# Each store as two transfers of 64 rows: a grouped 1x1 convolution on Trainium2

## The chip, the cores and the metric

The kernel runs on one core of a Trainium2 chip. The metric is the device time of one execution in microseconds (us). Before the change it is 492.37 us (median of 2 runs, 492.31 and 492.43).

## The reference, cut to what matters

The input is an image of 512 x 512 pixels with 192 bf16 channels. The kernel size is 1, so each of four groups of 48 channels is multiplied by its own 48 x 48 matrix (shortened, with k = 1 filled in):

```python
H = W = 512; G = 4; Cg = 48; C = 192; k = 1
xg = xp.reshape(B, H, W, G, Cg)
out = out + jnp.einsum('bhwgc,gcd->bhwgd', xg, w[0, 0])     # once, as k = 1
```

That is 100.7 MB in and 100.7 MB out with little arithmetic.

## The kernel before

Pixels are laid out so that each of the 128 partitions holds a contiguous run of pixels. The 2048 pixel columns per partition are moved in pieces. Most have 64 columns, which is 3 MB: 128 rows of 24,576 bytes. At both ends there are five smaller pieces. SP (SyncE) issues the loads, ACT (ScalarE) the stores. TensorE (PE) transposes pixels, multiplies them by the weights, and writes to PSUM; DVE (VectorE) copies the transposed data, and ACT and DVE evict the results, that is, copy them from PSUM to SBUF. Input and output each have a ring of 256 columns, four pieces. A piece of the output ring may be overwritten only when its store has landed, that is, when its semaphore has reached the count that the code waits for, 16 for each store (the trace has 16 landings for each).

```python
def rows_view(ap, p):
    return ap[128 * p.col:128 * (p.col + p.size), :].rearrange("(p i) c -> p (i c)", p=128)
...
for p in stores:
    seen[p.key] = seen.get(p.key, 0) + 16
    st_val[p] = seen[p.key]
...
def wait_out_free(wq, g):                      # ACT and DVE, before an eviction
    if g >= body:                              # body: 64 groups, the whole ring
        p = store_at[g - body]
        wq.wait(st_sem[p.key], st_val[p])
...
# SP
for p in loads:
    wq.wait(t_done, p.g1 - body)
    sp.dma_start(ring_view(x_sb, p), rows_view(xf, p)).then_inc(ld_sem[p.key], 16)
...
# ACT
def store(p):
    act.dma_start(rows_view(of, p), ring_view(o_sb, p)).then_inc(st_sem[p.key], 16)

for g in range(NG):
    wait_out_free(wq, g)
    wq.wait(mm_done, g + 1)
    while pending and pending[0][1] <= g:
        store(pending.pop(0)[0])
    ...                                        # evict group g
    if g in store_end:
        pending.append((store_end[g], g + ST_DELAY))
```

Of the kernel before, what the change touches and what calls it, by code (L numbers as in the profile page):

```python
# [67 lines left out]
def bass_standalone__grouped__vision_kernel(nc, x, w, out):  # L68
# [14 lines left out]
    of = out.rearrange("b h w c -> (b h w) c")  # L83
# [9 lines left out]
    def shared(g):  # L93
        return g % 4 == 1 and g < NG - 3
# [9 lines left out]
    def rows_view(ap, p):  # L104
        return ap[128 * p.col:128 * (p.col + p.size), :].rearrange("(p i) c -> p (i c)", p=128)

    def ring_view(t, p):
        at = p.col % RCOLS
        assert at + p.size <= RCOLS
        return t[:, at * C:(at + p.size) * C]  # L110

    with ExitStack() as es:
        block = es.enter_context(nc.Block())
        x_sb = es.enter_context(nc.sbuf_tensor("x_sb", [128, RCOLS * C], BF16))
        o_sb = es.enter_context(nc.sbuf_tensor("o_sb", [128, RCOLS * C], BF16))
# [8 lines left out]
        def sem(name):  # L124
            return es.enter_context(nc.semaphore(name))

        ld_sem = {k: sem(f"ld_{k[0]}{k[1]}") for k in dict.fromkeys(p.key for p in loads)}
        st_sem = {k: sem(f"st_{k[0]}{k[1]}") for k in dict.fromkeys(p.key for p in stores)}
        st_val, seen = {}, {}
        for p in stores:  # L130
            seen[p.key] = seen.get(p.key, 0) + 16
            st_val[p] = seen[p.key]
        w_sem, id_sem, e_sem, wb_sem, wc_sem = (sem(s) for s in ("w_sem", "id_sem", "e_sem", "wb_sem", "wc_sem"))
        p0_sem, p1_sem = sem("p0_sem"), sem("p1_sem")
# [5 lines left out]
        def wait_out_free(wq, g):  # L140
            if g >= body:
                p = store_at[g - body]
                wq.wait(st_sem[p.key], st_val[p])

        @block.gpsimd
        def _(gp):
            gp.memset(esel[:], 1.0).then_inc(p0_sem, 1)  # L147
            gp.memset(ident[:], 1.0).then_inc(p1_sem, 1)  # L148
            gp.wait_ge(p0_sem, 1)
            gp.affine_select(out=esel[:], in_=esel[:], pattern=[[-1, ECOLS]],  # L150
                             compare_op=AluOpType.is_equal, fill=0.0, base=ESHIFT,
                             channel_multiplier=1).then_inc(e_sem, 1)
            gp.wait_ge(p1_sem, 1)
            gp.affine_select(out=ident[:], in_=ident[:], pattern=[[-1, 128]],  # L154
                             compare_op=AluOpType.is_equal, fill=0.0, base=0,
                             channel_multiplier=1).then_inc(id_sem, 1)
# [101 lines left out]
        @block.scalar  # L258
        def _(act):
            wq = Waiter(act)  # L260
            pending = []

            def store(p):
                act.dma_start(rows_view(of, p), ring_view(o_sb, p)).then_inc(st_sem[p.key], 16)  # L264

            for g in range(NG):
                wait_out_free(wq, g)
# [3 lines that stand above are left out]
                v = 2 * g  # L271
                u = g % body * 2
                if shared(g):
                    ins = act.copy(o_sb[:, u * UC:(u + 1) * UC], o_ps[:, v % NOB, 0:UC])  # L274
                else:
                    dst = o_sb[:, u * UC:(u + 2) * UC].rearrange("p (u c) -> p u c", u=2)
                    ins = act.copy(dst, o_ps[:, v % NOB:v % NOB + 2, 0:UC])  # L277
                ins.then_inc(fa_sem[g % RING], 1)
                if g in store_end:
                    pending.append((store_end[g], g + ST_DELAY))  # L280
            for (p, _) in pending:
                act.wait_ge(fa_sem[(p.g1 - 1) % RING], 1)
                store(p)
            for p in stores:
                if st_val[p] == seen[p.key]:
                    wq.wait(st_sem[p.key], st_val[p])
# [28 lines left out]
```

## Time and profile before

| | before |
|---|---|
| time, span of the profiled run | 492.37 us, 489.8 us |
| bytes moved | 201.6 MB |
| middle of the run (106 to 425 us) | DMA share 1.00, 431 GB/s |
| a row of 24,576 bytes | one packet, 912 ns (median), so 26.9 GB/s in each of 16 engines |
| store issues on ACT | 40 of 338 ns, 13.7 us in total |

The packet durations are from the trace's records of single packets, which the views below only sum up. From the page of the kernel before: the DMA share and rate in 40 slices of the span, the two queues (packets, MB, share of 16 engines' time; q1 has the loads, q10 the stores), the chain that ended last by engine and by line, and the large issues (count, KB, us to landing).

```profile
span 489.8 us, 14171 instructions
...
DMA  8999999999999999999999999999999999998593
GB/s 297 430 425 423 428 430 433 427 435 425 436 425 432 433 431 433 429 432 431 425 433 430 429 435 429 434 429 433 429 429 426 438 421 434 421 424 351 238 385 149
...
q1 hardware_dynamic: 5968, 100.68, 48.3%
q10 hardware_dynamic: 5760, 100.67, 48.2%
...
DMA 77%; PE 18%; ACT 1%; another core or an unknown queue 1%; issue 1%; SPq 1%; ACTq 0%
DMA out_dram<-o_sb 73%; PE o_ps L215 10%; PE xT_ps L192 8%; DMA x_sb<-in_x_dram 4%; ACT o_sb L277 1%; SPq L164 0%; ACTq L264 0%; SPq L161 0%; ACTq L46 0%
...
out_dram<-o_sb ACTq DMA_DIRECT2D x30, 3072.0 KB, 45.4
```

The DMA slices stay at 9 of 10 nearly to the end, at about 430 GB/s, with loads and stores half each. The chain is 73% stores. A store takes 45.4 us to land, though 3 MB alone would take 7.3 us at 431 GB/s: it stands in a queue behind earlier stores (in the middle they land 15.2 us apart, three in its 45.4), and shares the engines with loads (48.3% and 48.2% of their time).

The stretches view gives, for stretches of the span, the busy time of each engine, then the granted PE clock, the DMA share and the rate:

```profile
106.00:425.00 319.00, 277.20 (x4032) 268.47 (x4032) 221.08 (x421) 233.49 (x337) 0.00 (x0) 0.95 1.00 431
...
460.00:490.00 30.00, 16.80 (x227) 15.53 (x226) 10.99 (x21) 15.07 (x21) 0.00 (x0) 0.84 0.54 224
```

PE is busy for 277 of 319 us there and ACT for 233, so both have slack. DMA has none. Waits by engine (total us, times, longest) show what the queue does to the others:

```profile
ACT o_sb L277 <- DMA out_dram<-o_sb: 46.9, 23, 2.8
PE o_ps L215 <- ACT o_sb L277: 44.8, 25, 2.7
```

Last, ACT's timeline at one store (start, us; ACTq is its issue):

```profile
348.72 0.80 ACT L277 CAST o_sb<-o_ps 128x768 bf16<-128x768 f32 x1 [2.75 <-DMA out_dram<-o_sb]
348.73 0.34 ACTq L264 DMA_DIRECT2D out_dram<-o_sb  x1
```

ACT waited 2.75 us for a store to land. The issue of the next store took 0.34 us and ran under an eviction.

### The profile page before, as it was taken

What the parts mean: (1) busy time and instruction counts of PE and PEld (TensorE: products, weight loads), DVE (VectorE), ACT (ScalarE), POOL (GpSimd) and SP (SyncE); (2) the same over time, 40 slices, a digit from 0 to 9 for tenths busy, and PEclk for the clock granted to TensorE, in tenths of its full rate; (3) what the DMA queues carried; (4) which work ended last, traced back from release to release, by engine and by line L of the source; (5) the groups of instructions that cost most, each with busy time, mean ns of one, the idle gap of its engine ahead of it and who ended that gap; (6) DMA issues with size and microseconds to landing.
All of it is one profiled execution on the core that took longest, in us unless ns stands there. A gap on an engine that the chain in (4) does not pass through costs nothing.

```text
span 489.8 us, 14171 instructions
## 1 busy us (share of the span) xinstructions
PE 423.4 (86%) x6154; PEld 407.9 (83%) x6154; DVE 336.1 (69%) x640; ACT 357.2 (73%) x513; POOL 1.3 (0%) x8
## 2 busy tenths in 40 slices
PE   5999989977997979979798979899798979799962
PEld 5899989977987879878788878898787978799862
DVE  3688878867675767757676757767577757588750
ACT  2788878866785767767677757678586868688862
POOL 1000000000000000000000000000000000000000
PEclk9999999999898998989998989989899989899996
DMA  8999999999999999999999999999999999998593
GB/s 297 430 425 423 428 430 433 427 435 425 436 425 432 433 431 433 429 432 431 425 433 430 429 435 429 434 429 433 429 429 426 438 421 434 421 424 351 238 385 149
DMA packets 11750, 201.63 MB, mean 412 GB/s; under 512 B 1488, under 2 KB 2512, under 8 KB 3536
## 3 DMA queue, kind: packets, MB, share of 16 engines
q1 hardware_dynamic: 5968, 100.68, 48.3%
q10 hardware_dynamic: 5760, 100.67, 48.2%
q8 instruction: 12, 0.20, 0.1%
q14 instruction: 10, 0.08, 0.0%
HBM read 100.68 MB, written 100.66 MB: 411 GB/s over the span
## 4 chain that ended last, share of the span: by engine, by line
DMA 77%; PE 18%; ACT 1%; another core or an unknown queue 1%; issue 1%; SPq 1%; ACTq 0%
DMA out_dram<-o_sb 73%; PE o_ps L215 10%; PE xT_ps L192 8%; DMA x_sb<-in_x_dram 4%; ACT o_sb L277 1%; SPq L164 0%; ACTq L264 0%; SPq L161 0%; ACTq L46 0%
## 5 line engine op out<-in xcount | busy, mean ns | idle before, releaser
L277 ACT CAST o_sb<-o_ps 128x768 bf16<-128x768 f32 x385 | 301.7, 799 | 116.8 <-PE o_ps L215 68.4
L249 DVE COPY xT_sb<-xT_ps 128x768 bf16<-128x768 bf16 x512 | 284.0, 555 | 111.4 <-PE xT_ps L192 104.4
L215 PE MATMUL o_ps<-wt,xT_sb 128*128 128x144 bf16 (+1 forms) x3072 | 308.2, 238 | 47.9 <-ACT o_sb L277 44.8
L192 PE MATMUL xT_ps<-ident,x_sb 128*128 128x128 bf16 x3072 | 265.7, 225 | 7.8 <-DMA x_sb<-in_x_dram 7.3
L215 PEld LDWEIGHTS o_ps<-wt,xT_sb 128*128 128x128 bf16 x3072 | 217.8, 100 | 61.4 <-issue 52.5
L192 PEld LDWEIGHTS xT_ps<-ident,x_sb 128*128 128x128 bf16 x3072 | 205.6, 101 | 9.5 <-DMA x_sb<-in_x_dram 7.6
L255 DVE CAST o_sb<-o_ps 128x384 bf16<-128x384 f32 x127 | 69.8, 550 | 28.0 <-DMA out_dram<-o_sb 26.7
L274 ACT CAST o_sb<-o_ps 128x384 bf16<-128x384 f32 x127 | 61.0, 480 | 8.0 <-PE o_ps L215 5.1
L245 DVE CAST wt<-o_ps 128x480 bf16<-128x480 f32 x1 | 0.7, 658 | 3.2 <-PE o_ps L176 3.2
L176 PE MATMUL o_ps<-w_sb,esel 48*128 48x48 bf16 x10 | 0.6, 210 | 2.6 <-DMA w_sb<-in_w_dram 2.6
L176 PEld LDWEIGHTS o_ps<-w_sb,esel 48*128 48x128 bf16 x10 | 0.5, 112 | 2.5 <-POOL esel L150 2.5
L277 ACT ACT_TABLE_LOAD x1 | 1.3, 1283 | 0.8 <-PEq L300 0.8
L150 POOL TENSOR_SCALAR_AFFINE_SELECT esel<-esel 48x272 bf16<-48x272 bf16 x1 | 0.4, 406 | 0.0
L147 POOL MEMSET esel<- 48x272 bf16 x1 | 0.3, 318 | 0.3 <-POOLq L300 0.3
L154 POOL TENSOR_SCALAR_AFFINE_SELECT ident<-ident 128x128 bf16<-128x128 bf16 x1 | 0.3, 285 | 0.0
L148 POOL MEMSET ident<- 128x128 bf16 x1 | 0.2, 198 | 0.0
L300 POOL MEMSET const-bfloat16-1.0<- 128x1 bf16 x1 | 0.1, 102 | 0.0
L300 POOL MEMSET const-uint8-127<- 128x1 uint8 x1 | 0.1, 102 | 0.0
L300 POOL MEMSET const-float32-0.0<- 128x1 f32 x1 | 0.1, 98 | 0.3 <-issue 0.3
L300 POOL MEMSET const-float32-1.0<- 128x1 f32 x1 | 0.1, 98 | 0.0
## 6 DMA issues: line engine op xcount, KB each, us to landing
x_sb<-in_x_dram SPq DMA_DIRECT2D x30, 3072.0 KB, 25.7
out_dram<-o_sb ACTq DMA_DIRECT2D x30, 3072.0 KB, 45.4
x_sb<-in_x_dram SPq DMA_DIRECT2D x2, 1536.0 KB, 19.7
out_dram<-o_sb ACTq DMA_DIRECT2D x2, 1536.0 KB, 24.9
x_sb<-in_x_dram SPq DMA_DIRECT2D x2, 768.0 KB, 21.5
out_dram<-o_sb ACTq DMA_DIRECT2D x2, 768.0 KB, 20.0
x_sb<-in_x_dram SPq DMA_DIRECT2D x4, 192.0 KB, 27.2
x_sb<-in_x_dram SPq DMA_DIRECT2D x2, 384.0 KB, 24.4
```

Source lines behind the costliest of these rows:

```text
L147: gp.memset(esel[:], 1.0).then_inc(p0_sem, 1)
L150: gp.affine_select(out=esel[:], in_=esel[:], pattern=[[-1, ECOLS]], compare_op=AluOpType.is_equal, fill=0.0, base=ESHIFT, channel_multipli ...
L154: gp.affine_select(out=ident[:], in_=ident[:], pattern=[[-1, 128]], compare_op=AluOpType.is_equal, fill=0.0, base=0, channel_multiplier=1) ...
L176: last = pe.matmul(o_ps[:, NOB - 1, col:col + CG], lhsT=esel[:, s0:s0 + 128], rhs=w_sb[:, g, :], start=True, stop=True, skip_group_check=True)
L192: ins.append(pe.transpose(xT_ps[:, g % NXP, j * 128:(j + 1) * 128], x_sb[:, col:col + 128], ident[:]))
L215: ins.append(pe.matmul(o_ps[:, v % NOB, c0_:c1_], lhsT=xs[:, j * 128:(j + 1) * 128], rhs=wt[:, WOFF[tc]:WOFF[tc] + (c1_ - c0_)], start=(tc ...
L245: dve.tensor_copy(wt[:], o_ps[:, NOB - 1, 0:WCOLS]).then_inc(wc_sem, 1)
L249: dve.tensor_copy(xT_sb[g % NXP][:], xT_ps[:, g % NXP, 0:2 * UC]).then_inc(e1_sem[g % RING], 1)
L255: dve.tensor_copy(o_sb[:, u * UC:(u + 1) * UC], o_ps[:, v % NOB, 0:UC]).then_inc(d2_sem[g // 4 % 2], 1)
L274: ins = act.copy(o_sb[:, u * UC:(u + 1) * UC], o_ps[:, v % NOB, 0:UC])
L277: ins = act.copy(dst, o_ps[:, v % NOB:v % NOB + 2, 0:UC])
L300: nc = _bacc.Bacc("TRN2", target_bir_lowering=False, num_devices=1)
```

## The change

Each store is issued as two transfers, rows 0 to 63 and rows 64 to 127, on the same queue. The intent of such a split is usually smaller units that start and finish separately. Here the wait still needs both.

```diff
         for p in stores:
-            seen[p.key] = seen.get(p.key, 0) + 16
+            seen[p.key] = seen.get(p.key, 0) + 32
             st_val[p] = seen[p.key]
...
             def store(p):
-                act.dma_start(rows_view(of, p), ring_view(o_sb, p)).then_inc(st_sem[p.key], 16)
+                for r in (0, 64):
+                    act.dma_start(rows_view(of, p)[r:r + 64, :], ring_view(o_sb, p)[r:r + 64, :]).then_inc(st_sem[p.key], 16)
```

## The prediction

> **What bounds the kernel now.** The 16 DMA engines. The page's slices show DMA at 0.9 or more from slice 2 to 37 and about 430 GB/s; the stretches view gives DMA share 1.00 and 431 GB/s from 106 to 425 us. The queue table splits it evenly: loads 48.3%, stores 48.2% of 16 engines. The chain of waits is 73% store transfers, in links of 45.5 us: a store is about three pieces deep in its queue, and its landing frees the output ring for ACT (46.9 us of waits) and DVE (26.7 us). A 24,576-byte row is one packet of 912 ns in the trace's DMA records: 26.9 GB/s per engine, 16 of them 431. PE (86%) and ACT (73%) have slack.
>
> **What the change does directly.** Bytes and row length stay the same, so data packets stay the same. Each store gets a second set of 16 completion packets: 640 more at 9 ns over 16 engines is 0.4 us. ACT issues 40 more transfers at 338 ns (13.5 us in total), where it idles 27%; I put 0 to 3 us of it on the chain. Completion is not earlier, since the wait needs both halves. There is nothing to gain.
>
> **What it does indirectly, the main term.** A 128-row store reads all of SBUF; a 64-row one reads half. [...] The trace before has no large 64-row transfer, so no run shows it yet. [...]
>
> Stores are half the traffic (215 GB/s)[...]. But an engine alternates load and store packets[...]. Let T be 0.91 us. A load and store pair takes 2T now; [...] engines that lag by over half a store (4 packet pairs, 7.3 us) read different halves. One engine already lands up to 20 us behind, the rest within 2 to 5 us. So I expect 1.15 to 1.4 times over the roughly 390 us in which both queues run, and some 5 to 15 us at the end, where only stores run.
>
> Estimate: 492 + 0.25 × 390 + 10 = 600 us. Range 494 to 710; the top is 1.5 times throughout. Faster 1%, within 2% 26%, slower 73%.
>
> **What would show it.** Right: store packets' mean well over 918 ns, towards 1.2 to 1.8 us, with load packets near 915; DMA share still near 1.0 in the middle but GB/s down to 290 to 380; PE and ACT idle more, waiting on stores; the store links of the chain longer than 45.5 us; the same number of data packets and 6,400 packets on the store queue. If the store packets stay at 912 ns, [...] the time should be within 1% of before.
>
> **What would make it wrong.** [...] the engines settling into opposite phases by themselves, load on one and store on the other.

The sum came to 600 us: 492 as measured, 0.25 × 390 = 98 for the middle, and 10 for the end. Terms are cut from the text, with the cuts marked: why a 64-row store should be slower, and the model that led to 1.15 to 1.4 times, to 1.5 times at the top and to the 5 to 15 us at the end. The 98 and the 10 us stand as estimates of mine without their ground. What I expected, that store packets of the same 64 adjacent rows slow each other down, was tested afterwards (e4_bench below: 1879 ns for a packet against 919).

## The result, and the profile after

The changed kernel takes 533.13 us (median of 2 runs, 529.41 and 536.86), 1.0835 times the kernel before, with a 95% interval from 1.0705 to 1.0966. Ratios here are the mean time of one kernel's fast runs over that of the other's of the same rounds. In the experiments the first, profiled run of each kernel is left out of them, so they are not quite the ratios of the medians quoted. The forecast of slower was right; the forecast size, 600 us, was not. The same page lines after the change:

```profile
span 535.0 us, 14211 instructions
...
DMA  8999999999999999999999999999999999999896
GB/s 319 425 425 423 400 367 379 399 395 399 407 375 412 404 391 404 402 353 386 404 412 413 408 375 401 418 410 406 423 410 369 401 417 391 365 320 233 200 231 202
...
q10 hardware_dynamic: 6400, 100.67, 52.8%
...
PE 49%; DMA 36%; issue 9%; ACT 3%; ACTq 2%; SPq 0%; another core or an unknown queue 0%
DMA out_dram<-o_sb 35%; PE o_ps L215 28%; PE xT_ps L192 21%; ACT o_sb L278 3%; ACTq L265 2%; DMA x_sb<-in_x_dram 1%; SPq L164 0%; SPq L161 0%; ACTq L46 0%
...
out_dram<-o_sb ACTq DMA_DIRECT2D x60, 1536.0 KB, 38.2
```

The DMA slices are as full as before, but they now move about 400 GB/s, and near the end only 200 to 230. The store queue has 640 more packets, as predicted, and its share of the engines' time has risen from 48.2% to 52.8% for the same bytes: packets take longer. The chain is no longer mostly stores; PE has 49% of it.

The stretches of the changed kernel, in the same columns, the first one as before and the second one its end:

```profile
106.00:425.00 319.00, 269.79 (x3805) 259.45 (x3802) 208.98 (x398) 219.77 (x316) 0.00 (x0) 0.93 1.00 399
...
482.00:535.00 53.00, 31.30 (x418) 28.71 (x415) 22.11 (x42) 26.48 (x38) 0.00 (x0) 0.81 0.84 215
```

The waits of the changed kernel (L275 and L278 are its evictions on ACT; "issue" is time for which the profile shows no releaser, and on ACT the next view shows the store issues in it):

```profile
ACT o_sb L275 <- issue: 71.3, 27, 4.1
...
ACT o_sb L278 <- DMA out_dram<-o_sb: 13.7, 10, 3.5
...
PEld o_ps L215 <- issue: 90.0, 53, 3.8
```

And ACT's timeline at one store of the changed kernel:

```profile
391.42 4.17 ACTq L265 DMA_DIRECT2D out_dram<-o_sb  x2
395.64 0.48 ACT L275 CAST o_sb<-o_ps 128x384 bf16<-128x384 f32 x1 [4.11 <-issue]
```

The rate in the middle went from 431 to 399 GB/s at a DMA share of 1.00. In the waits, ACT's wait for landed stores fell (46.9 to 13.7 us) and a new one came: 71.3 us of issue. The timeline shows it: two issues took 4.17 us and the eviction behind them stood for 4.11 us.

The packet records show why the rate fell. Between 106 and 425 us:

| packets of 24,576 bytes | load, mean ns | store, mean ns | stores over 1.1 x 912 ns |
|---|---|---|---|
| before | 910 | 917 | 0.7% |
| after | 943 | 1026 | 16.8% |

The records do not name the engine. But where the end of one row's packet fits one next start only (3,500 cases in this stretch before the change), 88% of the steps go from one queue to the other. So I take an engine to alternate load and store packets. A pair then costs 1969 ns in place of 1827, 1.078 times, and 431/399 is 1.080. Longer packets account for the whole loss of rate in the middle.

To place the loss in time, I take the moment at which 99% of the load bytes have landed. Before, that is at 439.8 us, and the stores end 49.2 us later. After, it is at 472.0 us and 62.2 us. So of the 45 us that the profiled spans differ by, 32 are lost while loads and stores run together and 13 in the rest. The second profile of the changed kernel (e5_after_again, below) gives 29 and 18 us, so this split holds to some 5 us only.

### The profile page after: what moved, and what is told of

It reads as the page before. It is cut to its first block, busy times and chain, and to the rows that moved or that the text cites. A ratio compares the mean times of both kernels' runs of the same rounds, so it can differ in the third digit from the quotient of the medians.

```text
span 535.0 us, 14211 instructions
## 1 busy us (share of the span) xinstructions
PE 437.9 (82%) x6154; PEld 419.4 (78%) x6154; DVE 337.0 (63%) x640; ACT 358.0 (67%) x513; POOL 1.3 (0%) x8
## 3 DMA queue, kind: packets, MB, share of 16 engines
q10 hardware_dynamic: 6400, 100.67, 52.8%
## 4 chain that ended last, share of the span: by engine, by line
PE 49%; DMA 36%; issue 9%; ACT 3%; ACTq 2%; SPq 0%; another core or an unknown queue 0%
DMA out_dram<-o_sb 35%; PE o_ps L215 28%; PE xT_ps L192 21%; ACT o_sb L278 3%; ACTq L265 2%; DMA x_sb<-in_x_dram 1%; SPq L164 0%; SPq L161 0%; ACTq L46 0%
## 5 line engine op out<-in xcount | busy, mean ns | idle before, releaser
L215 PE MATMUL o_ps<-wt,xT_sb 128*128 128x144 bf16 (+1 forms) x3072 | 316.2, 242 | 81.7 <-issue 64.5
L278 ACT CAST o_sb<-o_ps 128x768 bf16<-128x768 f32 x385 | 302.2, 799 | 79.9 <-PE o_ps L215 56.8
L215 PEld LDWEIGHTS o_ps<-wt,xT_sb 128*128 128x128 bf16 x3072 | 223.6, 102 | 98.8 <-issue 90.0
L192 PE MATMUL xT_ps<-ident,x_sb 128*128 128x128 bf16 x3072 | 271.3, 228 | 2.7 <-DMA x_sb<-in_x_dram 2.4
L192 PEld LDWEIGHTS xT_ps<-ident,x_sb 128*128 128x128 bf16 x3072 | 210.8, 102 | 3.7 <-DMA x_sb<-in_x_dram 2.0
L275 ACT CAST o_sb<-o_ps 128x384 bf16<-128x384 f32 x127 | 60.7, 478 | 90.0 <-issue 71.3
```

The source lines that it names most:

```text
L192: ins.append(pe.transpose(xT_ps[:, g % NXP, j * 128:(j + 1) * 128], x_sb[:, col:col + 128], ident[:]))
L215: ins.append(pe.matmul(o_ps[:, v % NOB, c0_:c1_], lhsT=xs[:, j * 128:(j + 1) * 128], rhs=wt[:, WOFF[tc]:WOFF[tc] + (c1_ - c0_)], start=(tc ...
L275: ins = act.copy(o_sb[:, u * UC:(u + 1) * UC], o_ps[:, v % NOB, 0:UC])
L278: ins = act.copy(dst, o_ps[:, v % NOB:v % NOB + 2, 0:UC])
```

## The experiments

The theory: packets of the same half of the partitions, 0 to 63 or 64 to 127, slow each other down, and those of transfers with rows in both halves do not. What in the hardware would do this, no run shows; a range that names no theory is this theory's. The rival: it is the number of transfers, and the time for which their issues hold ACT. Open beside these was why the loss was well under half of the forecast. Each whole kernel below was timed in three rounds beside the kernel before (492.0 to 492.4 us in the three sets of runs).

| run | what differs from the changed kernel | median us of fast runs | ratio to before | load, store packet in the middle, mean ns |
|---|---|---|---|---|
| e5_after_again | nothing | 534.17 | 1.0823 | 943, 1005 |
| e1_cols | cut by columns, all rows | 495.43 | 1.0082 | 932, 466 (half the size) |
| e6_evenodd | even rows, then odd rows | 492.70 | 1.0014 | 915, 917 |
| e2_onehalf | both transfers read partitions 0 to 63 | 573.20 | 1.1668 | 975, 1087 |
| e8_swap | order of halves swapped in every second piece | 552.89 | 1.1239 | 960, 1060 |
| e3_loads | loads in halves, stores whole | 574.64 | 1.1732 | 1078, 953 |
| e7_quarters | four transfers of 32 adjacent rows | 590.79 | 1.1995 | 1048, 1074 |
| e9_strided4 | four transfers of every fourth row | 525.76 | 1.0695 | 952, 917 |
| e10_swapq_whole | whole stores issued by SP, loads by ACT | 491.70 | 0.9979 | 910, 917 |
| e11_swapq_halves | the same, stores in halves | 525.16 | 1.0636 | 944, 1039 |

The ratio for e3_loads still contains its slow run; without it the ratio is 1.170.

### Which rows, or how many transfers: e1_cols and e6_evenodd

```diff
-                for r in (0, 64):
-                    act.dma_start(rows_view(of, p)[r:r + 64, :], ...
+                h = p.size * C // 2
+                for c in (0, h):                                       # e1_cols
+                    act.dma_start(rows_view(of, p)[:, c:c + h], ...
+                for r in (0, 1):                                       # e6_evenodd
+                    act.dma_start(rows_view(of, p)[r::2, :], ...
```

> Each store is still two transfers on the same queue, but cut by columns: 128 rows of 32 columns each (packets of 12,288 bytes), so each transfer reads all 128 partitions. [...] store packets near 460 ns with none long, time 488 to 498 us. Rival, transfer count (80 issues in place of 40, 1,280 completion packets, ACT held by a second issue of up to 3.7 us): as slow as the changed kernel, 525 to 540 us. If between 498 and 525, both have a part.

> Two transfers of 64 rows as in the changed kernel, same number, size, order and queue, but the even rows first and then the odd rows[...]. [...] store packets back to 912 to 930 ns, 490 to 498 us, within 1.5% of before. Transfer count or issue time on ACT: as slow as the changed kernel, 525 to 540 us.

Both met the theory. The even and odd rows are the cleanest run: the transfers have the same number, size, order and queue, and only the choice of rows differs (in SBUF and, with it, in DRAM; e2_onehalf below tells the two apart). The loss vanishes (1.0014, interval 0.9981 to 1.0047), and store packets are back at 917 ns. From the stretches of e6_evenodd:

```profile
106.00:425.00 319.00, 276.31 (x4042) 266.61 (x4039) 220.94 (x421) 234.40 (x338) 0.00 (x0) 0.96 1.00 430
```

Its store issues in the view by tensor (number, then shortest, median and longest in ns):

```profile
L265 ACTq DMA_DIRECT2D out_dram<-o_sb x80: 478/604/1542, 11.0 to 488.3; - x80
```

And those of the changed kernel:

```profile
L265 ACTq DMA_DIRECT2D out_dram<-o_sb x80: 472/615/3668, 11.1 to 532.3; - x80
```

Issues got longer in both (338 ns before), so a 64-row issue costs more than a whole one (medians 604 and 615 ns). The very long ones are in the changed kernel: in its trace the second issue of a store takes 1.95 us on average, against 0.71 us with even and odd rows. All issues take 99.5 us in the one and 47.9 us in the other. The 34 us more than before (13.7 us) cost e6_evenodd nothing. So the long issues come with the halves of adjacent rows and are not a price of the number of transfers. (With SP issuing, in e11_swapq_halves below, the second issue takes 1.80 us, so they do not depend on ACT. What makes an issue wait is not shown.)

The columns were within 1% but not equal to before (1.0082, interval 1.0043 to 1.012). Its rate in the middle is 424 GB/s. Its store packets are half as long as the load packets that they alternate with; I did not look for the cause of that 1%.

### The limit of one half by itself: e4_bench

This kernel computes nothing and gives a wrong result. It runs ten phases of plain transfers, each queued at once and ended by a wait.

```python
A, B = slice(0, 64), slice(64, 128)
ph.append([("act", "st", 4 + n, r, r, ...) for n in range(4) for r in (A, B)])       # halves in turn
ph.append([("act", "st", 8 + n, r, r, ...) for r in (A, B) for n in range(4)])       # A A A A B B B B
ph.append([("act", "st", 12 + n, r, r, ...) for n in range(4) for r in (even, odd)])
...
```

> Wrong result on purpose, no computing: ten phases of plain transfers of 12.6 MB in each direction used, each phase ended by a wait. [...] whole stores near 430 GB/s (29 us); 64-row halves in turn 215 to 300 GB/s; four first halves then four second halves close to 215 GB/s; even rows then odd rows faster than halves; first halves on one queue and second halves on the other 215 to 430; 64-row loads like 64-row stores [...]; loads beside whole stores 430 GB/s; loads beside 64-row halves 390 to 425; loads beside stores of partitions 0 to 63 only 290 to 390. [...]

(The case against the theory: every phase within 5% of 430 GB/s.)

Worked out from the packet records (bytes of a phase over the time from its first packet's start to its last one's end):

| phase | GB/s | mean packet, ns |
|---|---|---|
| stores, whole | 427 | 919 |
| stores, halves in turn | 241 | 1527 |
| stores, four first halves, then four second | 207 | 1879 |
| stores, even rows and odd rows in turn | 427 | 918 |
| stores, first halves on ACT's queue, second on SP's | 289 | 1370 and 1284 |
| loads, halves in turn | 208 | 1867 |
| loads beside whole stores | 418 | 942 and 922 |
| loads beside stores in halves | 379 | 1001 and 1016 |
| loads beside stores of partitions 0 to 63 only | 366 | 1028 and 1062 |

When four first halves are queued and then four second, so that all packets in flight are nearly always of one half, each packet takes twice as long (1879 ns on average against 919; the first sixteen took 1.77 to 1.92 us), and 16 engines move 207 GB/s. That is the limit of one half, seen alone; loads in halves, in turn, run at the same rate (208 GB/s). A transfer of 64 rows is not the trouble: even and odd rows run at full rate (427 GB/s). The phase with loads beside halves came out a little under the 390 that I expected at least. Beside loads, the same halves lose little (379 GB/s against 418), and that is the puzzle of the size.

### Why the loss was small: e12_bench2, e2_onehalf and e8_swap

The second run of transfers alone makes the phases longer (14 stores in the last one).

> Wrong result on purpose, no computing, all transfers of a phase queued at once. Phase 1: 4 whole loads beside 4 whole stores, near 430 GB/s. Phase 2: 7 loads beside 7 stores in halves. Phase 3: 7 loads beside 14 stores of partitions 0 to 63 only. Phase 4: 14 stores in halves, nothing beside them. If engines settle by themselves into opposite phases of load and store packets, the store packets' mean in the middle of phase 3 stays under 1050 ns, though no other half is to be had; random phases would give 1300 to 1400 ns. If they also get past each other by lag, phase 2 is faster than phase 3, and phase 4 goes from about 215 GB/s at its start to over 280 at its end.

One line of the page of e12_bench2, the rate in slices of 11 us. The last phase, phase 4, takes the slices from the one with 181, which it shares with a gap, to the end. The slice with 148 is still the end of phase 3:

```profile
GB/s 286 369 427 436 430 434 293 403 430 418 407 385 414 412 403 418 221 322 405 430 387 407 405 389 378 412 324 148 181 230 255 280 322 376 425 432 430 434 430 217
```

In the last phase, stores in halves with nothing beside them start at about 220 GB/s and climb to 430 without any change in what is issued. The landing records have 16 times for each transfer, which I take as one for each of the 16 engines. By them, the engines finish the first transfer of that phase within 0.2 us of each other. The spread then grows to 4.8 us at the seventh, and from the tenth to the last but one it is 3.2 to 3.7 us. Shared out evenly, 64 rows are four packets for each engine, 4 x 0.912 = 3.65 us at full speed, so the spread is about one whole half. I read this as engines that have moved apart until some read the first half while others read the second. This I call escape by lag. The starting rate, the climb and the spread are measured; that engines are on opposite halves is inferred, since the packet records do not name the engine.

Phase 3 of the same run leaves no second half to escape into. Over stretches of 10 us from 200 to 290 us, store packets average 929 to 1039 ns, against 1.37 us for random phases (917 ns and half of 912). That is an estimate of mine from e4_bench, where a store packet takes 1879 ns when the packets around it are of its half and 919 ns when they are of both halves: at random it would meet its half for half of the time. So the engines must mostly be out of step, some in a load packet while those that would slow them are in a store packet: opposite phases. This too is inferred, and which engines slow which is not shown. What brings them there, no run shows. When the loads of that phase have landed and its stores run alone, their packets average 1.79 us (298 to 308 us). Phase 2, with the other half to be had, is a little faster than phase 3 (388 against 366 GB/s, both with their ends), as expected.

In the kernel, the two were tested with one edit each:

```diff
-                    act.dma_start(rows_view(of, p)[r:r + 64, :], ring_view(o_sb, p)[r:r + 64, :])...
+                    act.dma_start(rows_view(of, p)[r:r + 64, :], ring_view(o_sb, p)[0:64, :])...   # e2_onehalf, wrong result on purpose
-                for r in (0, 64):
+                for r in ((0, 64) if p.col // BIG % 2 == 0 else (64, 0)):                           # e8_swap
```

> Wrong result on purpose: both transfers of a store read partitions 0 to 63, the second writes the output rows 64 to 127 all the same. Number, size and order of transfers as in the changed kernel. [...] engines escaping into opposite halves (why the slowdown was 8% and not 22%): there is no opposite half to escape to, so store packets' mean in the middle rises from 1026 ns to 1200 to 1400 ns and the time to 570 to 640 us. If the engines instead escape by opposite phases of load and store packets, it stays at 525 to 550 us. Transfer count theory: 525 to 540 us, the same as the changed kernel.

> The halves of every second piece are issued in the other order, so that the queue reads 0-63, 64-127, 64-127, 0-63: runs of eight packets on the same half instead of four (14.6 us instead of 7.3 us of alternating load and store packets). If engines get past each other by lagging into the other half, they now need twice the lag: store packets' mean in the middle goes from 1026 to 1050 to 1150 ns and the time up to 540 to 565 us. If opposite phases of load and store packets do it, the same time as the changed kernel within 1.5%. Transfer count theory: the same time too.

> The changed kernel once more, as the ruler for the three runs beside it. 525 to 540 us, ratio 1.07 to 1.10; store packets in the middle of the run 1000 to 1050 ns on average.

Without a second half the time rose to 573.20 us, inside the expected range, but the store packets did not reach 1200 ns: they average 1087. This run also answers a rival, that the order of rows in DRAM is what costs: it writes the same DRAM rows in the same order as the changed kernel and reads other SBUF rows, and that alone makes it 39 us slower. With runs of eight packets in place of four, over which engines would need twice the lag to be on different halves, it rose to 552.89 us and 1060 ns, as the lag theory said. Both ratios are clear of the interval of e5_after_again (1.0781 to 1.0865), though only e8_swap was timed in the same rounds as it. Counted as excess over 917 ns: random phases would give 456 ns, one half only gives 170, the swapped order 143, the changed kernel 88 to 109. By this count opposite phases save most, and lag a further part. It rests on the estimate for random phases, which no run switches on. Load packets, which the estimate leaves alone, grew too (by 65, 50 and 33 ns over 910); with them the excess is 235, 193 and 121 to 142 ns against 456. Lag is also seen in the kernel: between 106 and 425 us the first 15 engines to land a store transfer do so within 13.3 and 10.3 us (medians of the two profiles of the changed kernel), against 3.8 before. By itself that proves nothing, since e1_cols, whose transfers all read 128 partitions, has 9.6.

The same stretch of e2_onehalf:

```profile
106.00:425.00 319.00, 266.67 (x3690) 257.25 (x3688) 202.41 (x385) 213.93 (x309) 0.00 (x0) 0.91 1.00 380
```

And of e8_swap:

```profile
106.00:425.00 319.00, 269.92 (x3748) 260.74 (x3746) 204.92 (x390) 217.49 (x313) 0.00 (x0) 0.91 1.00 390
```

### Loads in halves: e3_loads

```diff
-                sp.dma_start(ring_view(x_sb, p), rows_view(xf, p)).then_inc(ld_sem[p.key], 16)
+                for r in (0, 64):
+                    sp.dma_start(ring_view(x_sb, p)[r:r + 64, :], rows_view(xf, p)[r:r + 64, :]).then_inc(ld_sem[p.key], 16)
...
-                    pe.wait_ge(ld_sem[p.key], 16)
+                    pe.wait_ge(ld_sem[p.key], 32)
...
```

("Share" in the last sentence of this expectation means: slow each other down.)

> Stores whole as before; each load is issued as two transfers of 64 rows, by the queue of SP, which computes nothing. Transfer count holding ACT: nothing is added on ACT, so 490 to 496 us. [...] load packets get long (mean in the middle 1000 to 1100 ns, from 914) and the time is 515 to 545 us. If only reads share, load packets stay near 915 ns and the time within 1% of before.

Nothing was added on ACT, and the kernel became slower than the changed one, 574.64 us. So the halves of adjacent rows cost time without ACT's issues, and in writes into SBUF as in reads from it (load packets of 1078 ns here against 910). The loss was larger than expected, in part because of the start of the run, which I had left out. Two stretches of e3_loads:

```profile
20.00:64.00 44.00, 31.01 (x421) 30.01 (x419) 23.10 (x45) 24.02 (x35) 0.00 (x0) 0.84 1.01 232
106.00:425.00 319.00, 258.04 (x3586) 247.98 (x3583) 196.88 (x375) 210.97 (x301) 0.00 (x0) 0.91 1.00 389
```

From 20 to 64 us nearly only loads run, and they move 232 GB/s where the kernel before moves 426, its stores included. Loads in halves with nothing beside them did not climb in e4_bench either: each of its eight transfers landed 7.4 to 7.5 us after the one before, the last as the first, and the spread of the engines stayed at 1.3 to 1.4 us. Why stores escape there and loads do not is open.

### What ACT's hold costs: e7_quarters, e9_strided4, e10_swapq_whole, e11_swapq_halves

```diff
-                for r in (0, 64):
-                    act.dma_start(rows_view(of, p)[r:r + 64, :], ring_view(o_sb, p)[r:r + 64, :])...
+                for r in (0, 32, 64, 96):                                       # e7_quarters
+                    act.dma_start(rows_view(of, p)[r:r + 32, :], ring_view(o_sb, p)[r:r + 32, :])...
+                for r in range(4):                                              # e9_strided4
+                    act.dma_start(rows_view(of, p)[r::4, :], ring_view(o_sb, p)[r::4, :])...
```

(The semaphore counts go up with the number of transfers; those lines are cut.)

> Four transfers of 32 rows for each store: twice the transfers and issues of the changed kernel[...]. [...] near the changed kernel, 525 to 550 us, ratio within 3% of the run beside it. Transfer count theory: the excess doubles, 565 to 585 us, with ACT held by issues for 140 us or more in place of 71.

> Four transfers of 32 rows for each store, as in the run with quarters (591 us), but each takes every fourth row (0, 4, 8, ... then 1, 5, 9, ... and so on)[...]. Number, size and queue as in the quarters. [...] 490 to 500 us, store packets' mean under 940 ns, second and later issues well under the 1.0 us of the quarters. Transfer count theory, which the quarters met: 565 to 600 us again.

The quarters came out slower than either theory said (590.79 us), with ACT standing 131.5 us for issues in the waits, and would have pointed to the number of transfers. The strided quarters, with the same number and size, are 65 us faster and their store packets are clean at 917 ns, so most of the quarters' loss comes with adjacent rows again. But e9_strided4 missed both ranges too: 525.76 us is 34 us over before. The 160 issues take 98.7 us in all, load packets are 952 ns for a reason that I did not find, and the kernel ends on its compute. The chain of e9_strided4 by engine:

```profile
PE 81%; issue 13%; ACTq 2%; DMA 1%; ACT 1%; SPq 0%
```

And that of e5_after_again, the second profile of the changed kernel:

```profile
PE 80%; issue 15%; ACTq 1%; DMA 1%; ACT 1%; SPq 0%
```

In the waits of e9_strided4, ACT stands 86.8 us for issues, and PE, which had slack before (14% of the span), is now on the chain that ends last. In the second profile of the changed kernel the chain is on PE as well; in the first, PE had 49% and DMA 36%. I read this as two limits that lie close together: slow packets, and PE waiting for an ACT that is held. (PE was also busy for longer, 438 us against 423, at a mean granted clock of 0.92 against 0.96; I did not test that apart.) To take the second away, the queues were exchanged: SP, which computes nothing, issues the stores, and ACT the loads, whole (lines shortened):

```diff
 @block.sync
+            for p in stores:
+                wq.wait(mm_done, p.g1 + ST_DELAY)          # the last two wait for their evictions
+                sp.dma_start(...)                          # e10: whole; e11: two of 64 rows
 @block.scalar
-                while pending and pending[0][1] <= g:
-                    store(pending.pop(0)[0])
+                load(g)                                    # the loads that group g has made room for
```

> Control for the next run. Whole stores, issued by SP, which computes nothing; loads, whole, issued by ACT between its evictions. 488 to 500 us.

> As the control, but each store is two transfers of 64 rows, issued by SP: ACT never waits in a store issue (in the changed kernel it was held for 71 us). If the long issues [...] cost nothing, 525 to 545 us, 1.07 to 1.10 times the control. If holding ACT is what costs, 490 to 505 us, within 2% of the control; in between, both.

The control is as fast as before (491.70 us). The halves cost 1.0636/0.9979 = 1.066 there, against 1.082 with ACT issuing. The profiled spans of the pair differ by 35 us. The time to 99% of the load bytes grows by 33 us (440.8 to 473.6), as in the changed kernel, and the rest by 2 us (48.3 to 50.2), where in the changed kernel it grows by 13 or 18.

The middle stretch of e11_swapq_halves:

```profile
106.00:425.00 319.00, 264.73 (x3755) 256.32 (x3753) 205.85 (x391) 217.22 (x314) 0.00 (x0) 0.92 1.00 396
```

So the 32 us of the middle need no held ACT. Most of the loss at the end goes when ACT is not held. This was "in between, both", nearer to the theory that the issues cost nothing. Exchanging the queues also moves the loads. So the split, 33 us for the adjacent halves and some 10 us for ACT's hold (45 or 47 us less 35), is an estimate from these profiles.

The waits changed with it. With SP issuing, ACT's wait for landed stores rose from 36.9 us in e10_swapq_whole to 62.0 in e11_swapq_halves, as one would expect of slower stores. In the changed kernel ACT stands in its issues instead, and little of this wait is left.

## Why the prediction was right or wrong

- **"The 16 DMA engines" bound the kernel, and "There is nothing to gain"**: right. Even and odd rows, columns and whole stores from SP all end within 1% of before.
- **Direct costs**: the 640 completion packets were right in number (6,400 packets) and cost nothing that e6_evenodd shows. The issues were undersized. I put "0 to 3 us" on the chain from 338 ns each. They took 0.53 and 1.95 us on average in a pair, 99.5 us in all, and cost about 10 us (estimate above).
- **That stores of 64 adjacent rows are slowed**: right, and shown: 207 GB/s with one half in flight at a time, against 427 for whole stores, and no loss with even and odd rows (427).
- **The step that failed: "1.15 to 1.4 times" over 390 us, about 98 us at the centre.** It measured 1.078 times in the middle, and 32 us (29 in the second profile). The direction was right and this term was three times too large. It was an estimate of mine: I took the phases of the engines to be random, which says nothing of what slowed engines do next. The runs point to two ways out, both inferred: opposite phases of load and store (e12_bench2, phase 3: 929 to 1039 ns in the middle where random phases would give 1.37 us by my estimate) and lag into the other half (573 us without another half, 553 us when twice the lag is needed, 534 us as changed). The prediction named both, opposite phases only as a way to be wrong and lag only in passing.
- **The end**: "5 to 15 us" was predicted, 13 us measured, and 18 in the second profile. The reason given was half rate where only stores run (241 against 427 GB/s in e4_bench). The rate in the kernel alone does not show it (215 GB/s from 482 to 535 us, but 224 before from 460 to 490, where the engines were idle half the time); the DMA share does, 0.84 against 0.54. But with stores issued by SP the end grew by 2 us only. The size was about right; the reason was at best a part, so the size was in part luck.
- **What would show it**: store packets over 918 ns, a DMA share near 1.0 and packet counts were right; "1.2 to 1.8 us" and "290 to 380" GB/s were the same overestimate (1.026 us, 399 GB/s). Load packets rose to 943 ns, which I had put "near 915". The waits were wrong: ACT and PE were to wait more on stores, but ACT's wait on them fell from 46.9 to 13.7 us, and 71.3 us of its own issues took its place. The store links of the last chain are 44.6 to 48.8 us, but there are four of them where there were eight. (The prediction's reading of the landings was also rough: in the middle the last engine is up to 21.9 us behind and the rest within 2.2 to 8.2.)

## What to carry to other kernels

Cut a transfer so that each part still has rows in both halves of the partitions: by columns (1.0082 times before here), or by every second row (1.0014), but not into partitions 0 to 63 and 64 to 127 (1.0835). And cut no finer than needed: four parts of every fourth row still cost 34 us. When a resource is shared by streams that alternate, don't multiply a worst case or a random case through the run: streams that slow each other can move out of each other's way (stores in halves climbed from about 220 to 430 GB/s by themselves in e12_bench2), so measure the conflict alone and in the mixture. And read how long issues hold the engine that makes them: here they grew with the conflict (338 ns for a whole store, 1.95 us on average for the second of two halves), and they held an engine that had looked free.
